# Batch 1's first head pair loaded alone ahead of the output weights, and visits and transposes of token tile 0 placed anew

## Chip, cores and metric

The kernel runs on one core of one Trainium2 chip. The metric is the device time of one execution in microseconds, the lower the better. The kernel before takes 364.70 us (median of 3 executions, 364.70 to 365.26).

## The reference

Block-causal attention for 8 batches of 8 heads (576 tokens, head size 64), then a feed-forward layer with a gated ReLU on the 4608 tokens. Cut to what matters:

```python
scores = q @ k.T / sqrt(64)                 # per batch and head, 576 x 576
scores = where(block_i >= block_j, scores, -1e9)   # blocks of 64 tokens
attn = softmax(scores) @ v
x = attn, heads side by side                # 4608 x 512
out = (relu(x @ w_gate) * (x @ w_val)) @ w_out     # 512 -> 1536 -> 512
```

## The kernel before: the parts that matter

TensorE does everything that can be done as a matmul, and is meant never to stand still. The feed-forward layer goes through the tokens in tiles of 512 (tile 0 is batch 0's first 512 tokens, tile 1 batch 1's, and so on). While TensorE works on tile 0, the attention of batch 1 is put in between its matmuls. The places are given by hand: each matmul of a tile is a step, 144 to a tile. Steps 0 to 95 of a tile are the gate and value products, steps 96 to 143 the output product. An event `(p, f)` puts `f` before step `p`.

The heads go in pairs. Batch 1 has the pairs r = 4, 5, 6, 7; its pair number inside the batch is `hp` = 0, 1, 2, 3. (The prediction says "pair 1's k" and "pair 2" by `hp`, and "visits 5, 6, 7" and "pair 7" by r.) For each pair:

1. `mains_1(hp)`: TensorE transposes q and k into PSUM; VectorE copies q out (`qTm`) and ScalarE copies k out (`kTm`).
2. The visit: TensorE makes the scores, ScalarE takes exponentials of them (two of 128x256, two of 128x1024).
3. `head_av` twice, or `both_av`: the products with v; VectorE normalises each head (a reciprocal and a multiplication).
4. `pe_xT`: TensorE transposes the result, ScalarE (for pair 7 VectorE) copies it out as `xT`, which the next tile reads.

The last 64 tokens of a batch (the 576 are 512 and 64) are its *tail*; they have transposes and visits of their own, which matter here only by their places in tile 1 (`pe_tails`). A *running sum* is one that TensorE is still adding up in PSUM.

```python
psum_sc  = tile_pool(bufs=2)   # scores
psum_one = tile_pool(bufs=1)   # one bank
psum_ffn = tile_pool(bufs=3)   # three banks, shared by the feed-forward sums, one
                               # 128x256 piece of a visit's scores, head_av, transposes
# ... cut
def round_at(p, r, av, to_xT, after=(6, 13)):
    # visit r at step p, products with v at av, transposes at to_xT[0]
    # ... cut
def mains_1(hp):
    if hp == 3:
        both = psum_one.tile([128, 1024], BF, name="one")
        # ... cut
    e1.pe_mains(hp, (dve, act), two)

# loads, in order of issue on SyncE's queue
e1.load_qk(0, 4)                               # q, k of pairs hp 0 and 1: 1 MB
ffn(24)
w_out = [load_w_out(i) for i in range(3)]      # wo: 3 MB
e1.load_v(0, 4)
for h0 in (4, 6):
    e1.load_qk(h0, 2)                          # hp 2, hp 3
e1.load_v(4, 4)
# ... cut
events = round_at(96, 4, (122, 122.1), (126, pe_xT), (6, 11))
events += round_at(112, 5, (130, 130.1), (136, pe_xT), (4, 14))
events += round_at(127.5, 6, (140, 141), (146, pe_xT), (4, 9))
events += round_at(140.5, 7, (150.5, None), (155, pe_xT), (3, 8))
```

The loads come as 32-bit numbers into staging buffers; GpSimd, and in some places VectorE and ScalarE, cast them to bf16.

The softmax here doesn't subtract the row's maximum and nothing guards it: scores larger than these inputs give would overflow.

## Time and profile before

| | before |
|---|---|
| time, median | 364.70 us |
| TensorE busy | 98% |
| granted clock of TensorE | full in all slices |
| start of the scores of visits 4, 5, 6, 7 | 39.38, 43.85, 49.75, 54.89 us |
| start of visit 8 (batch 2) | 74.62 us |
| gaps over 0.12 us in the matmul stream, 30 to 64 us | 2.32 us |
| last matmul's start to the end | 3.72 us |

The granted clock is the share of the full clock that TensorE was allowed, as the profile records it.

Where I give a gap, it is worked out from the records of the trace: the start of one matmul to the start of the next, less 0.417 ns for each column of the first (512 columns 0.213 us). The 0.417 is this trace's own: matmuls of 128 and of 512 columns that follow each other without a wait start 0.056 and 0.216 us apart (medians), 0.160 us for 384 columns. The busy time of matmuls cannot show it, since each record is longer (0.38 us) than its distance to the next.

From the page of the kernel before, the busy times (engine, us, share of the span, instructions), and the rows of TensorE and its clock in 40 slices, in tenths:

```profile
PE 355.3 (98%) x2965; PEld 176.1 (49%) x2965; DVE 168.2 (46%) x394; ACT 168.8 (47%) x280; POOL 112.3 (31%) x147
PE   7999999999999999999999999999999999999996
PEclk9999999999999999999999999999999999999999
```

TensorE runs at full clock and is the limit for most of the span (before 47 us the loads are too, as the result shows). The chain of waits of the same kernel (the work that ended last, followed back from the last instruction to whatever released each step; start, us, what) has near its end:

```profile
297.22 20.72 PE ffnp L593 x96
317.94 10.36 PE ffnp L678 x48
```

96 matmuls in 20.72 us are 0.216 us each: nothing shorter is seen in this trace, so I expect no gain there. What is to be gained lies in the first 64 us. TensorE's timeline of the kernel before (start, us, engine, line, operation, what from what, how many; in brackets the idle time and what ended it) around the output product of tile 0:

```profile
40.03 3.88 PE L678 MATMUL ffnp<-wo,hT 128*128 128x512 bf16 x16
43.85 0.28 PE L399 MATMUL one<-qTm,kTm 64*128 64x256 bf16 x1
...
44.50 2.53 PE L678 MATMUL ffnp<-wo,hT 128*128 128x512 bf16 x10
47.22 0.47 PE L512 MATMUL one<-v_bf,attnT 128*128 128x65 bf16 x10 [0.19 <-POOL v_bf L181]
```

Sixteen matmuls would take 3.46 us, but the next group starts 3.82 us later. 0.1 of the difference is the switch to matmuls of 64 rows, which is found at every visit; 0.26 is a wait for a cast of wo in the middle of the group. The ten that follow lose 0.20 in the same way, and 0.36 (0.19 of it beyond the last matmul's own record) before the first product with v, L512. And at the start of tile 1:

```profile
58.43 0.77 PE L512 MATMUL sc<-v_bf,attnT 128*128 128x65 bf16 x20
59.63 0.61 PE L593 MATMUL sc<-xT,wv 128*128 128x512 bf16 x2 [0.43 <-DVE xnat L478]
...
60.95 0.38 PE L593 MATMUL sc<-xT,wv 128*128 128x512 bf16 x1
61.62 0.59 PE L593 MATMUL ffnp<-xT,wg 128*128 128x512 bf16 x2 [0.30 <-DVE xT L559]
```

Twenty products of 65 columns last 0.60 us, so the next matmul could start at 59.04; it starts 0.59 us later, since it writes to the scores' PSUM buffer that VectorE's normalisation of pair 7 (L478) still reads. Then 0.46 us pass until pair 7's `xT` is there.

### The profile page before, as it was taken

To read this page: it belongs to the slowest core of one execution; us is meant where nothing else is said; L and a number is where in the kernel's file an instruction comes from. 1 tells how busy PE (TensorE), PEld (TensorE's weight loads), DVE (VectorE), ACT (ScalarE), POOL (GpSimd) and SP (SyncE) were. 2 spreads that over 40 slices of the span, in tenths; PEclk is the share of its full clock that TensorE was granted. 3 is DMA by queue.
4 is the path that set the end of the run, shared out by engine and by line. 5 is a ranking of instruction groups with operands and counts; after the bars stand their busy time and mean duration, and the time that the engine had idled before them with its cause. 6 is when DMAs were issued, how large, how long until landed. Compare 5 with 4: busy or idle time off the path is not lost.

```text
span 362.9 us, 7464 instructions
## 1 busy us (share of the span) xinstructions
PE 355.3 (98%) x2965; PEld 176.1 (49%) x2965; DVE 168.2 (46%) x394; ACT 168.8 (47%) x280; POOL 112.3 (31%) x147
## 2 busy tenths in 40 slices
PE   7999999999999999999999999999999999999996
PEld 3644455554554455444544454445544454444443
DVE  4844465566534443554454434543455434333432
ACT  5853655587046643663256624564355333302310
POOL 6756656489138100850057003900000000000000
PEclk9999999999999999999999999999999999999999
DMA  8999999999999992999389963999100420031014
GB/s 254 286 357 374 310 220 293 198 110 174 177 205 123 143 170 81 80 132 177 117 56 144 147 134 55 143 136 152 64 17 14 74 81 0 0 89 29 0 39 108
DMA packets 150387, 49.58 MB, mean 137 GB/s; under 512 B 132816, under 2 KB 143312, under 8 KB 150352
## 3 DMA queue, kind: packets, MB, share of 16 engines
q0 software_dynamic: 70320, 8.85, 52.1%
q1 hardware_dynamic: 74944, 31.47, 42.2%
q10 hardware_dynamic: 5088, 8.78, 7.6%
q8 instruction: 23, 0.38, 0.4%
q14 instruction: 12, 0.10, 0.1%
HBM read 37.75 MB, written 9.44 MB: 130 GB/s over the span
## 4 chain that ended last, share of the span: by engine, by line
PE 85%; DMA 9%; SPq 2%; POOL 1%; DVE 0%; issue 0%; ACT 0%; POOLq 0%; ACTq 0%
PE ffnp L593 46%; PE ffnp L678 24%; PE ffnp L512 5%; DMA stage<-in_k_dram 4%; PE sc L399 3%; DMA stage<-in_moe_w_val_dram 3%; PE ffnp L492 3%; DMA stage<-in_v_dram 3%; SPq L139 2%; PE one L399 2%; PE sc L433 1%; POOL v_bf L181 0%; PE one L433 0%; PE one L593 0%; PE ffnp L260 0%
## 5 line engine op out<-in xcount | busy, mean ns | idle before, releaser
L609 DVE TENSOR_TENSOR hT<-gate_sb,ffnp 128x512 bf16<-128x512 bf16 x106 | 72.7, 687 | 100.5 <-PE ffnp L593 72.1
L603 ACT ACTIVATE gate_sb<-ffnp 128x512 bf16<-128x512 f32 x103 | 61.8, 602 | 88.5 <-PE ffnp L593 88.5
L678 PE MATMUL ffnp<-wo,hT 128*128 128x512 bf16 (+2 forms) x444 | 101.5, 373 | 0.1
L593 PE MATMUL ffnp<-xT,wv 128*128 128x512 bf16 x376 | 99.9, 379 | 0.0
L593 PE MATMUL ffnp<-xT,wg 128*128 128x512 bf16 x364 | 98.2, 379 | 0.4 <-DVE xT L559 0.3
L593 PEld LDWEIGHTS <-wg 128*128 128x128 bf16 x432 | 40.0, 98 | 46.1 <-issue 3.5
L593 PEld LDWEIGHTS <-wv 128*128 128x128 bf16 x432 | 39.8, 98 | 45.3 <-issue 2.3
L678 PEld LDWEIGHTS <-hT 128*128 128x128 bf16 x444 | 40.5, 98 | 42.9 <-issue 1.7
L408 ACT ACTIVATE attnT<-sc 128x1024 bf16<-128x1024 f32 x56 | 56.9, 1039 | 0.0
L282 POOL DMA_DIRECT2D q_bf<-in_q_dram x20 | 17.7, 900 | 92.0 <-DVE hT L609 78.4
L688 DVE COPY ob<-ffnp 128x512 f32<-128x512 f32 (+2 forms) x37 | 25.0, 677 | 40.2 <-PE ffnp L678 40.1
L512 PEld LDWEIGHTS <-attnT 128*128 128x128 bf16 x640 | 25.9, 98 | 15.6 <-DVE xnat L478 3.8
L414 ACT ACTIVATE attnT<-one 128x256 bf16<-128x256 f32 x28 | 10.7, 384 | 35.8 <-PE ffnp L399 35.3
L477 DVE RECIPROCAL recip<-ffnp 128x4 f32<-128x4 f32 (+1 forms) x72 | 12.9, 180 | 29.7 <-PE ffnp L512 20.2
L512 PE MATMUL ffnp<-v_bf,attnT 128*128 128x65 bf16 x560 | 26.1, 194 | 0.0
L478 DVE TENSOR_TENSOR xnat<-ffnp,recip 128x256 bf16<-128x256 f32 x56 | 23.8, 425 | 1.9
L282 POOL DMA_DIRECT2D v_bf<-in_v_dram x25 | 21.3, 898 | 1.3 <-PE ffnp L593 1.0
L454 ACT ACTIVATE attnTt<-one 64x256 bf16<-64x256 f32 x8 | 3.0, 378 | 35.7 <-PE ffnp L433 35.7
L282 POOL DMA_DIRECT2D k_bf<-in_k_dram x20 | 17.7, 927 | 0.2 <-issue 0.2
L399 PE MATMUL sc<-qTm,kTm 64*128 64x512 bf16 (+1 forms) x168 | 16.9, 305 | 0.0
L399 PEld LDWEIGHTS <-kTm 64*128 64x128 bf16 x224 | 9.1, 94 | 14.8 <-issue 11.3
L445 ACT ACTIVATE attnTt<-sc 128x1024 bf16<-128x1024 f32 x16 | 15.7, 1014 | 0.0
(97 smaller groups left out, 251.6 us busy)
## 6 DMA issues: line engine op xcount, KB each, us to landing
out_dram<-ob ACTq DMA_DIRECT2D x29, 256.0 KB, 3.1
stage<-in_moe_w_gate_dram SPq DMA_DIRECT2D x6, 512.0 KB, 9.0
stage<-in_moe_w_val_dram SPq DMA_DIRECT2D x6, 512.0 KB, 9.1
stage<-in_moe_w_out_dram SPq DMA_DIRECT2D x6, 512.0 KB, 10.2
q_bf<-in_q_dram POOLq DMA_DIRECT2D x20, 128.0 KB, 5.4
k_bf<-in_k_dram POOLq DMA_DIRECT2D x20, 128.0 KB, 6.1
v_bf<-in_v_dram POOLq DMA_DIRECT2D x20, 128.0 KB, 7.1
stage<-in_v_dram SPq DMA_DIRECT2D x19, 128.0 KB, 5.0
```

Source lines behind the costliest of these rows:

```text
L282: ins = nc.gpsimd.dma_start(dst, src[b, :, 128 * c : 128 * c + n, :].rearrange("h p d -> p h d"),)
L399: nc.tensor.matmul(where[c].rearrange("p (c n) -> p c n", n=128), kTm[b % 2][head_of(hh), c, hp, :], qTm[b % 2][head_of(hh), c:4, hp, :], ...
L408: return lambda: nc.scalar.activation(at[:, :, lo : lo + 512], sc, AF.Exp, scale=scale)
L445: return lambda: nc.scalar.activation(at[:, :, 2 * i : 2 * i + 2, 0:256], main[i].rearrange("p g (h n) -> p g h n", h=2), AF.Exp, scale=scale,
L477: nc.vector.reciprocal(recip, av[:, :, 64])
L478: nc.vector.tensor_tensor(out=out, in0=av[:, :, 0:64], in1=recip.to_broadcast([rows, n, 64]), op=AX.mult,)
L512: nc.tensor.matmul(av[:, p, :], at[:, col : col + 128], v_bf[b % 2][:, c, h, :], start=(p == 0), stop=(c == p), skip_group_check=True,)
L593: nc.tensor.matmul(to, (wg, wv)[t][f // 4][:, c, 128 * (f % 4) : 128 * (f % 4) + 128], x[:, c], start=(c == 0), stop=(c == 3),)
L603: nc.scalar.activation(gate_sb, gate, AF.Relu)
L609: nc.vector.tensor_tensor(out=h, in0=gate_sb, in1=val, op=AX.mult)
L678: nc.tensor.matmul(op, hT[f][:, 128 * s : 128 * (s + 1)], wo[f // 4][:, f % 4, n0:n1], start=(f == 0), stop=(f == 11),)
L688: nc.vector.tensor_copy(ob, op)
```

## The change

Its intent: wo, for which TensorE waits, shall land earlier; q and k of the second and third pair, which are needed later, go behind it; and the visits are moved to fit. Pair 7, whose result tile 1 waits for, is finished two steps sooner.

```diff
-        e1.load_qk(0, 4)
+        e1.load_qk(0, 2)
         ffn(24)
         w_out = [load_w_out(i) for i in range(3)]
+        e1.load_qk(2, 2)
+        e1.load_qk(4, 2)
         e1.load_v(0, 4)
-        for h0 in (4, 6):
-            e1.load_qk(h0, 2)
+        e1.load_qk(6, 2)
         e1.load_v(4, 4)
 # ... cut: the casts in the same order; q and k of pair 1 cast on their own
-            if hp == 3:
+            if hp >= 2:
                 both = psum_one.tile([128, 1024], BF, name="one")
-            e1.pe_mains(hp, (dve, act), two)
+            e1.pe_mains(hp, (dve, dve if hp == 2 else act), two)
-        events = round_at(96, 4, (122, 122.1), (126, pe_xT), (6, 11))
-        events += round_at(112, 5, (130, 130.1), (136, pe_xT), (4, 14))
-        events += round_at(127.5, 6, (140, 141), (146, pe_xT), (4, 9))
-        events += round_at(140.5, 7, (150.5, None), (155, pe_xT), (3, 8))
+        events = round_at(96, 4, (129, 129.1), (135, pe_xT), (6, 11))
+        events += round_at(124, 5, (136, 136.1), (141, pe_xT), (4, 9))
+        events += round_at(131, 6, (142, 143), (146, pe_xT), (4, 9))
+        events += round_at(139, 7, (148, None), (153, pe_xT), (3, 8))
-            (92, lambda: mains_1(1)),
-            (123.5, lambda: mains_1(2)),
-            (132.5, lambda: mains_1(3)),
+            (117, lambda: e1.cast_qk(2, 2, (None, dve))),
+            (120, lambda: mains_1(1)),
+            (126, lambda: mains_1(2)),
+            (134, lambda: mains_1(3)),
 # ... cut: the first product of pair 4 goes to psum_ffn instead of psum_one
-            (16, lambda: e0.pe_tails((dve, act))),
-            (20, lambda: e1.pe_tails((dve, act))),
+            (20, lambda: e0.pe_tails((dve, act))),
+            (22, lambda: e1.pe_tails((dve, act))),
```

More of the change, by code (lines that the diff above doesn't have):

```diff
@@ L527, in head_av @@
         xnat = xnats[r]
-        if (b > 0 or hh == 1) and (r, hh) != (4, 0):
+        if b > 0 or hh == 1:
             av = psum_ffn.tile([128, 4, 65], FP, name="ffnp")
@@ L821 @@
         cast_w(halves[:1], pool)
-        e1.cast_qk(0, 4, (pool, None))
+        e1.cast_qk(0, 2, (pool, None))
         cast_w(w_out[0], pool)
@@ L827 @@
         cast_w(last_w[:1], pool)
+        e1.cast_qk(2, 2, (pool, None))
+        e1.cast_qk(4, 2, (pool, pool))
         e1.cast_v(0, 4, pool)
-        for h0 in (4, 6):
-            e1.cast_qk(h0, 2, (pool, pool))
+        e1.cast_qk(6, 2, (pool, pool))
         e1.cast_v(4, 4, pool)
@@ L923, in mains_1 @@
                 ]
-            e1.pe_mains(hp, (dve, act), two)
-        events = round_at(96, 4, (122, 122.1), (126, pe_xT), (6, 11))
-        events += round_at(112, 5, (130, 130.1), (136, pe_xT), (4, 14))
-        events += round_at(127.5, 6, (140, 141), (146, pe_xT), (4, 9))
-        events += round_at(140.5, 7, (150.5, None), (155, pe_xT), (3, 8))
+            e1.pe_mains(hp, (dve, dve if hp == 2 else act), two)
[3 more added lines that the diff above has]
+        events += round_at(139, 7, (148, None), (153, pe_xT), (3, 8))
         events += [
             (67, lambda: cast_w(halves[1:], act)),
-            (80, lambda: e1.cast_qk(0, 4, (None, dve))),
+            (80, lambda: e1.cast_qk(0, 2, (None, dve))),
             (90, lambda: mains_1(0)),
-            (92, lambda: mains_1(1)),
             (112.05, lambda: cast_w(last_w[1:], dve)),
-            (123.5, lambda: mains_1(2)),
-            (132.5, lambda: mains_1(3)),
+            (117, lambda: e1.cast_qk(2, 2, (None, dve))),
+            (120, lambda: mains_1(1)),
+            (126, lambda: mains_1(2)),
+            (134, lambda: mains_1(3)),
             (128, lambda: mains_2(0)),
```

## The prediction

("The skill" in it is the Trainium skill.)

> **What bounds it now.** TensorE's matmul stream: busy 98% (table of busy times), 85% of the chain of waits. From 297 us on that chain has 96 matmuls of 512 columns in 20.72 us, 0.216 us each, back to back; the Trainium skill (TensorE: Matmul & The Clock Gate, "Back-to-back issue gap") gives the same 216 ns. The granted clock is full in all slices. So only time in which the stream stands still can be won. From the starts of successive matmuls in TensorE's timeline I find about 5 us of that before 20 us (untouched), about 2.3 us between 37 and 63 us, and later nothing but 0.1 us at each switch between 128-row and 64-row matmuls.
>
> The 2.3 us: 0.18 (k transpose of batch 1's second pair waits for its PSUM bank), 0.26 and 0.20 (output product waits for the casts of wo rows f=6 and f=10), 0.36 (first product with v, at 47.2 us, waits for GpSimd's cast of v), 0.59 (token tile 1 waits for VectorE's normalisation of pair 7), 0.46 and 0.26 (tile 1 waits for xT of pair 7).
>
> **What the change does.** Bytes and matmuls stay; a 512-column k cast costs VectorE about 0.43 us, a 1024-column one 0.69. It moves things:
> - wo lands one q/k pair earlier: 512 KB, 1.4 to 1.5 us at the 350 to 385 GB/s of those slices. The two wo waits (0.46) should nearly vanish; but TensorE gets there earlier too, as visit 5 and pair 1's transposes no longer stand before it, so f=10 may still wait 0.2.
> - v lands about 1.5 us later, cast done near 48.6; its first product moves from step 122 to 129, near 48.5. A wait of 0.0 to 0.4 remains. (v comes in 256-byte pieces; the skill, DMA: Bandwidth & Descriptors, "Specifications", asks 512 B for line rate, and GB/s does dip to 220 at 45 to 54 us.)
> - Pair 7's normalisation and xT come two steps, 0.43 us, earlier relative to tile 1: its waits (1.31) should fall to about 0.3.
> - Visits 5, 6, 7 are squeezed from steps 112, 127, 140 to 124, 131, 139. Each gives ScalarE 2.5 us of exponentials (0.28+0.28+0.98+0.98). With the copies of kTm and xT (0.5 each) ScalarE gets about 10 us of work in the 10.5 us before tile 1; VectorE gets both copies of pair 2 (0.6 each). New waits: pair 1's k and visit 5 on VectorE's late cast and copy (0.3 each); the products of pairs 5 and 6 on PSUM buffers that ScalarE frees late (up to 1 and 0.5).
>
> **On the critical path.** Taken away: about 1.9 us. Newly made: 1 to 2.5 us. Walking both instruction orders with durations, rates and landing delays read from the trace (an estimate) gives +0.1 to +0.5 us; that walk overstates the present kernel's small waits. I take about 0.
>
> **Predicted: 364.6 us, 8 in 10 between 363.5 and 365.8. Faster by over 2%: 0.01; within 2%: 0.98; slower by over 2%: 0.01.**
>
> **What would show it.** The wo waits near 42 and 45 us gone or 0.2; v's cast starting near 47.6; the gap at the start of tile 1 under 0.3; new gaps of 0.3 to 1 us before the products of pairs 5 and 6, ScalarE busy almost without break from 46 to 57 us. After 64 us both timelines alike, shifted by under 1 us.
>
> **What would make it wrong.** ScalarE keeping up (then 363.3); v landing much later than one pair's time; staging buffers coming free later and holding back batch 2's loads, which would show after 60 us.

## The result

| | before | changed |
|---|---|---|
| time, median | 364.74 us | 365.57 us |
| lowest to highest | 364.70 to 365.26 (4) | 365.43 to 365.79 (4) |
| ratio to before | | 1.002, 95% interval 1.0003 to 1.0037 |
| start of visits 4, 5, 6, 7 | 39.38, 43.85, 49.75, 54.89 | 38.84, 46.51, 50.04, 54.91 |
| start of visit 8 | 74.62 us | 74.99 us |
| gaps over 0.12 us, 30 to 64 us | 2.32 us | 2.51 us |
| last matmul's start | 359.18 us | 359.55 us |
| last matmul's start to the end | 3.72 us | 4.07 us |

A ratio is the mean time of one kernel's runs over the mean of the other's runs of the same rounds, so it is not quite the ratio of the medians. Executions over 1.5% slower than the fastest of the same kernel are left out of the means. The changed kernel is 0.8 us slower, 0.2%: the same by the measure of 2%, but outside the spread of the undisturbed runs. The difference of the two profiled executions, 0.72 us, has two parts: 0.37 us until visit 8, which then stays as it is to the last matmul, and 0.35 us after the last matmul.

The page of the changed kernel shows nothing of it (PE still 98%, the clock full):

```profile
PE 355.1 (98%) x2965; PEld 175.4 (48%) x2965; DVE 168.7 (46%) x396; ACT 168.4 (46%) x279; POOL 112.6 (31%) x148
PE   6999999999999999999999999999999999999995
```

**The first part: the matmul stream.** From the first feed-forward matmul (16.25 and 16.27 us) to visit 8 both traces have 522 matmuls. Before this takes 58.37 us with 2.32 us in gaps over 0.12, after 58.72 us with 2.64. So the account closes: the old waits were replaced by new ones that are 0.3 us longer. (0.13 of the 2.64 lies before 30 us. Of the 2.32, 1.5 us were taken away and 0.8 stayed; 1.7 us are new.)

The chain of waits shows something that the prediction passed over. Its last load in the kernel before, and then in the changed one, with the cast that follows:

```profile
40.40 5.57 DMA stage<-in_v_dram
46.11 1.06 POOL v_bf L181
```

```profile
33.06 9.57 DMA stage<-in_moe_w_out_dram
42.69 0.88 POOL wo L340
```

Up to 47.17 us in the kernel before, it is the landing of v that sets the time. So, as I read the chain, TensorE's waits ahead of that (0.18, 0.26 and 0.20) could not be won by themselves; without them TensorE would have waited longer for v. Only what it waits after the last load on the chain is lost for certain.

TensorE's timeline of the changed kernel, for the stretch that answers to that of before:

```profile
39.49 5.57 PE L678 MATMUL ffnp<-wo,hT 128*128 128x512 bf16 x24
44.90 0.39 PE L239 MATMUL sc<-ident,q_bf 128*128 128x128 bf16 x4
...
48.05 0.81 PE L678 MATMUL ffnp<-wo,hT 128*128 128x512 bf16 x3
48.91 0.77 PE L512 MATMUL ffnp<-v_bf,attnT 128*128 128x65 bf16 x20
...
52.66 0.46 PE L512 MATMUL ffnp<-v_bf,attnT 128*128 128x65 bf16 x10
53.85 0.48 PE L512 MATMUL ffnp<-v_bf,attnT 128*128 128x65 bf16 x10 [0.74 <-DVE xnat L478]
...
56.74 0.38 PE L678 MATMUL ffnp<-wo,hT 128*128 128x512 bf16 x1
57.33 0.46 PE L512 MATMUL ffnp<-v_bf,attnT 128*128 128x65 bf16 x10 [0.21 <-ACT xT L559]
```

The output product waits for wo once, 0.22 us. The first product with v waits 0.21. But between the two heads of pair 5 TensorE now stands for 0.90 us, and before the second head of pair 6 for 0.38. At the start of tile 1, the waits that the change was after are nearly gone: the sc sum comes 0.16 us after its place, and no wait for pair 7's `xT` is left. But tile 1 begins at 57.85, and two new waits lie in its first steps: 0.25 before pair 6's transposes (58.53) and 0.18 before pair 7's products (59.38). So its first steps wait 0.59 us in all, where they waited 1.31.

```profile
58.53 0.40 PE L558 MATMUL one<-ident,xnat 128*128 128x128 bf16 x4
...
59.38 0.78 PE L512 MATMUL sc<-v_bf,attnT 128*128 128x65 bf16 x20
60.00 0.60 PE L593 MATMUL ffnp<-xT,wv 128*128 128x512 bf16 x2
60.59 0.61 PE L593 MATMUL sc<-xT,wv 128*128 128x512 bf16 x2
```

What holds TensorE between the heads of pair 5 is seen in the timeline of VectorE and ScalarE in the changed kernel:

```profile
52.33 0.69 DVE L248 COPY qTm<-one 128x512 bf16<-128x512 bf16 x1
53.06 0.58 ACT L248 COPY kTm<-one 128x512 bf16<-128x512 bf16 x1 [1.07 <-DVE qTm L248]
53.16 0.18 DVE L477 RECIPROCAL recip<-ffnp 128x4 f32<-128x4 f32 x1
53.37 0.42 DVE L478 TENSOR_TENSOR xnat<-ffnp,recip 128x256 bf16<-128x256 f32 x1
53.54 0.59 ACT L559 COPY xT<-ffnp 128x512 bf16<-128x512 bf16 x1
```

The last of the first head's products starts at 52.92; VectorE normalises them until 53.79; the second head starts at 53.85. So the second head writes into the very PSUM buffer that the first head has just left, and waits for a full round trip through VectorE. (The records name the semaphores too: the second head's first weight load waits for S101, which VectorE's normalisation updates, and not for S106, which ScalarE's copies update.) Another of the three `psum_ffn` buffers was not to be had, as I read the code: one holds the running output sum, the other the transposes of pair 4, which ScalarE copies out until 54.13 only, because its copy of `kTm` stood in front, which itself waited for VectorE's `qTm`. Before the second head of pair 6 it is ScalarE's copy: it copies out pair 5's `xT` at 56.68, behind an exponential, though the transposes were issued from 56.00 on, and TensorE goes on at 57.33:

```profile
55.77 1.03 ACT L408 ACTIVATE attnT<-sc 128x1024 bf16<-128x1024 f32 x1
56.68 0.61 ACT L559 COPY xT<-ffnp 128x512 bf16<-128x512 bf16 x1
```

This second reading was not tested alone; in e7, where VectorE makes that copy, the gap is gone, but places were moved there too.

ScalarE has become fuller in this stretch, but it is not full. From the table of stretches (length, then busy us and instructions of each engine, clock, DMA share, GB/s), before and after:

```profile
46.00:57.00 11.00, 10.81 (x128) 6.59 (x127) 6.91 (x21) 7.09 (x13) 7.40 (x11) 1.00 0.86 201
```

```profile
46.00:57.00 11.00, 10.22 (x120) 5.88 (x119) 6.04 (x18) 8.18 (x15) 6.57 (x10) 1.00 0.85 201
```

The columns after the length are PE, PEld, DVE, ACT and POOL: ACT goes from 7.09 to 8.18 us of 11, PE from 10.81 to 10.22. ScalarE even stands idle for 1.07 us just before its copy of `kTm`, waiting for VectorE. So what makes its copy of `xT` late is the order in its queue, and not that it has too much to do. By the releasers in the trace, four of the five gaps from 53 to 61 us (0.90, 0.25, 0.18, 0.16) end with VectorE, and 0.38 with ScalarE.

**The second part: the end.** What SyncE waits for after 358 us, before and after (engine, line, what for: us, times, longest):

```profile
SPq L1006 <- DMA out_dram<-ob: 1.2, 2, 1.0
SPq L1006 <- PEq L1006: 0.7, 2, 0.5
```

```profile
SPq L1009 <- DMA out_dram<-ob: 1.6, 1, 1.6
SPq L1009 <- PEq L1009: 0.6, 2, 0.5
```

L1006 and L1009 are the same place, the end of the program. Before, SyncE waits for stores in two pieces; after, in one piece. The records of SyncE there (us after the start of the last matmul, and the hardware DMA semaphore that the wait names; the first wait names none) show why:

```
before   1.15 -   1.22 S100  1.28 S102  1.34 S103  1.40 S104  2.41 S105  2.47 S107  2.75 S108  2.82 S109
changed  1.15 -   2.75 S100  2.81 S102  2.88 S103  2.94 S104  3.00 S105  3.06 S107  3.12 S108  3.18 S109
```

SyncE closes the program with nine waits in a fixed order, 0.06 us each. The last two stores end at the same time in both kernels (the wait that they end is at 2.75). Before, they signal S108 and S109, the last of the row, and one wait follows. After, they signal S100 and S102, and seven follow. The DMAs on the hardware queues take the eight semaphores in turn. The kernel before issues 168 of them, the changed one 170.

### The profile page after: what moved, and what is told of

It is laid out like the page before. It is cut to its first block, busy times and chain, and to the rows that moved or that the text cites. A ratio compares the mean times of both kernels' runs of the same rounds, so it can differ in the third digit from the quotient of the medians.

```text
span 363.6 us, 7469 instructions
## 1 busy us (share of the span) xinstructions
PE 355.1 (98%) x2965; PEld 175.4 (48%) x2965; DVE 168.7 (46%) x396; ACT 168.4 (46%) x279; POOL 112.6 (31%) x148
## 4 chain that ended last, share of the span: by engine, by line
PE 86%; DMA 10%; SPq 1%; ACT 1%; DVE 0%; POOL 0%; issue 0%; POOLq 0%
PE ffnp L593 46%; PE ffnp L678 25%; PE ffnp L512 5%; PE sc L399 3%; DMA stage<-in_moe_w_gate_dram 3%; PE ffnp L492 3%; DMA stage<-in_moe_w_out_dram 3%; DMA stage<-in_moe_w_val_dram 3%; PE one L399 2%; SPq L139 1%; DMA stage<-in_v_dram 1%; PE sc L433 1%; DMA stage<-in_k_dram 1%; PE one L433 0%; PE sc L593 0%
```

## The experiments

The theories at the start: **S**, the order of loads does what it should, and its gain is eaten because the visits are squeezed, so that PSUM buffers come back late, above all from ScalarE's queue. **L**, late v costs the time. **T**, the gain at the start of tile 1 only mirrors waits earlier. **D**, the moved transposes of the tails matter. **E**, the 0.35 us at the end hang on the number of DMAs alone. The experiments ran in three sets (e0 to e3, e4 to e7, e8 to e11), each on one chip with its own runs of the kernel before. Some executions there were disturbed (2 to 6 us longer, most of them at a mean clock of 0.994 to 0.998). All but two of them count, so the intervals of the ratios are wide and most contain 1; where they do, I read the medians, the lowest times, and the traces. The traces' gaps at PSUM buffers repeat within 0.05 us where neither their places nor their copies were changed; the waits for wo do not (0.46 in the kernel before, none in e5, which has the same stream; 0 to 0.32 in the changed kernel and its variants). The profiled executions of e3 and e7 are disturbed ones (365.62 and 368.50 us): they stand still for over 2 us near 110 and 111 us, after the stretch that is read here. Comparisons between sets are between chips. The places in e6, e7 and e11 were found by the walk of dependences that the prediction describes; the chip's runs decide.

In the table, the last column is the time from the last matmul's start to the end.

| run | this, median (lowest) | before on that chip, median (lowest) | ratio, 95% interval | visit 8 | gaps 30 to 64 us | end |
|---|---|---|---|---|---|---|
| e0 changed again | 365.77 (365.33) | 365.16 (364.45) | 1.000, 0.996 to 1.004 | 74.73 | 2.42 | 4.07 |
| e1 kTm of pair 7 by VectorE | 365.33 (365.09) | same | 1.0008, 0.9959 to 1.0056 | 74.26 | 1.98 | 4.07 |
| e2 new places, old loads | 366.71 (366.53) | same | 1.0026, 0.9986 to 1.0066 | 75.90 | 3.50 | 3.69 |
| e3 pair 7's part alone | 364.05 (363.60) | same | 0.9969, 0.9916 to 1.0023 | 73.52 | 1.01 | 3.73 |
| e4 changed, six more stores | 365.07 (364.96) | 364.69 (364.51) | 1.0021, 0.9996 to 1.0046 | 74.70 | 2.26 | 3.70 |
| e5 before, two more stores | 365.11 (364.82) | same | 1.0029, 0.9993 to 1.0066 | 74.48 | 1.86 | 4.07 |
| e6 before, mended | 363.84 (363.56) | same | 0.9976, 0.9964 to 0.9988 | 73.85 | 1.43 | 3.71 |
| e7 changed, mended | 364.65 (364.25) | same | 1.0012, 0.9979 to 1.0045 | 74.06 | 1.70 | 3.71 |
| e8 changed, old tail places | 365.70 (365.42) | 364.97 (364.60) | 1.0015, 0.9982 to 1.0047 | 74.83 | 2.72 | 4.06 |
| e9 v ahead of pair 2 | 366.17 (365.97) | same | 1.0024, 0.9993 to 1.0056 | 75.51 | 3.30 | 4.07 |
| e10 xT of pair 4 by VectorE | 365.57 (365.37) | same | 1.0010, 0.9973 to 1.0047 | 74.53 | 1.88 | 4.07 |
| e11 before, mended again | 363.65 (363.53) | same | 0.9958, 0.9933 to 0.9984 | 73.61 | 1.23 | 3.70 |

All outputs were correct.

### e0: the changed kernel again

No edit.

> The changed kernel once more, in five rounds, so that the experiments beside it have it on their own chip. Its loss against the kernel before was 0.8 us in time, but the two traces are only 0.37 us apart up to the last matmul. If the rest (0.4 us after the last matmul) is chance, the difference measured here falls towards 0.4 us; if it belongs to the change, it stays at 0.8 us.

Median 0.6 and lowest 0.9 us above the kernel before; the end is 4.07 us again. So the end belongs to the change. Visit 8 is 0.11 us later than in the trace of the kernel before; in the first trace of the changed kernel it was 0.37. Chance lies there: the gaps over 0.12 us sum up to 2.42 us here, to 2.64 in the first execution (0.13 of which, before 30 us, is missing here).

### e1: the k copy of pair 7 by VectorE

```diff
-            e1.pe_mains(hp, (dve, dve if hp == 2 else act), two)
+            e1.pe_mains(hp, (dve, dve if hp >= 2 else act), two)
```

> The changed kernel, with the one copy of kTm of head pair 3 of batch 1 given to VectorE instead of ScalarE. Theory S (the gain was eaten by ScalarE: its queue stands behind that copy, which waits for VectorE, and so the xT copy of pair 4 frees its PSUM buffer late): the gap of 0.90 us between the two heads' products of pair 5, near 52.9 us, shrinks to about 0.3, and the kernel gains 0.5 to 0.7 us over the changed one. Rival L (the order of the loads costs the time: v comes late and holds back what follows): nothing about v changes here, so the kernel stays within 0.2 us of the changed one, and the time won before pair 5 is lost again at a later wait.

The gap at 52.8 us fell from 0.90 to 0.32, visit 8 came 0.47 us sooner than in e0, and the median and the lowest time fell by 0.44 and 0.24 us. Theory S named the place and the size of the gap; the time won is less than the 0.5 to 0.7 us expected. Visit 8 comes 0.36 us sooner than in the kernel before, with the feed-forward matmuls starting at the same time (16.22 and 16.25): 0.58 us less in this one gap more than undoes the loss of the stream. TensorE's, ScalarE's and VectorE's timeline of this kernel:

```profile
52.45 0.58 ACT L559 COPY xT<-ffnp 128x512 bf16<-128x512 bf16 x1 [0.67 <-PE ffnp L558]
52.46 0.46 PE L512 MATMUL ffnp<-v_bf,attnT 128*128 128x65 bf16 x10
52.85 0.68 DVE L248 COPY kTm<-one 128x512 bf16<-128x512 bf16 x1
53.08 0.46 PE L512 MATMUL ffnp<-v_bf,attnT 128*128 128x65 bf16 x10 [0.16 <-ACT xT L559]
...
53.65 0.43 DVE L478 TENSOR_TENSOR xnat<-ffnp,recip 128x256 bf16<-128x256 f32 x1
```

With the copy of `kTm` out of its queue, ScalarE copies pair 4's `xT` at 52.45 instead of 53.54. And now the second head waits for that copy, no longer for the first head's normalisation: it starts a full microsecond before that normalisation ends (54.08), and its records name S106, ScalarE's semaphore. So the program was built with another buffer for it, the one of pair 4's transposes.

### e2: the new places with the old loads

The loads and casts are in the order of the kernel before (pairs 0 and 1 together ahead of wo, cast together); the events are those of the changed kernel without the separate cast at step 117.

> The changed kernel's places for visits, transposes and products, with the loads and casts in the order of the kernel before (pairs 0 and 1 loaded and cast together ahead of wo, then wo, v, pairs 2, 3). Rival L: v is 1.5 us earlier than in the changed kernel and the wait before its first product is gone, so this is as fast as the changed kernel or faster. Theory S: the two halves of the change belong together. The new places let TensorE reach the output product earlier, while wo lands as late as before, so the two waits for wo grow from 0.26 and 0.20 to about 0.9 and 0.5 us, the ScalarE waits stay (0.9 and 0.4), and the kernel is 1.0 to 1.5 us slower than the changed one.

0.9 us slower than e0 in the median, 1.17 us later at visit 8. The waits for wo are 0.20 and 0.98 (I had them as 0.9 and 0.5: in sum 1.18 instead of 1.4), the pair 5 and 6 gaps are again 0.90 and 0.38. So the new order of loads is worth about a microsecond to the new places, and L is wrong in its strong form. The end, 3.69 us, is that of the old loads: 168 DMAs.

### e3: pair 7's part alone, on the kernel before

```diff
-        events += round_at(140.5, 7, (150.5, None), (155, pe_xT), (3, 8))
+        events += round_at(139, 7, (148, None), (153, pe_xT), (3, 8))
-            (16, lambda: e0.pe_tails((dve, act))),
-            (20, lambda: e1.pe_tails((dve, act))),
+            (20, lambda: e0.pe_tails((dve, act))),
+            (22, lambda: e1.pe_tails((dve, act))),
```

> The kernel before, with only the last part of the change: visit 7 at step 139, its products at 148, its transposes at 153, and the transposes of the tails at 20 and 22. Theory S: here ScalarE has room, so the gain that the changed kernel shows at the start of token tile 1 (waits of 0.59, 0.46 and 0.26 us down to 0.2 to 0.3 in all) is kept, with about 0.4 us of new wait at visit 7; 0.6 to 0.9 us faster than the kernel before. Rival T (the start of tile 1 is not where the changed kernel gains; its gain there only mirrors waits earlier): within 0.2 us of the kernel before.

1.1 us below the kernel before in the median, 0.85 in the lowest; visit 8 at 73.52 instead of 74.62. Of the three waits at the start of tile 1 (1.31 us) 0.16 is left, and 0.35 is new before visit 7. Rival T falls. These few lines take away 1.15 of the 1.5 us that the whole change takes away. TensorE's timeline of e3 around the new wait and the start of tile 1:

```profile
54.36 0.28 PE L399 MATMUL one<-qTm,kTm 64*128 64x256 bf16 x1 [0.18 <-ACT kTm L248]
...
58.52 0.60 PE L593 MATMUL ffnp<-xT,wv 128*128 128x512 bf16 x2
59.12 0.60 PE L593 MATMUL sc<-xT,wv 128*128 128x512 bf16 x2
```

Part of the 1.1 us is chance: in this execution the waits for wo did not show, because the feed-forward matmuls started at 16.53 instead of 16.25, and the loads were no later for it. The trace of e5 below allows for that: it has the stream of the kernel before, also started late (16.64) and shows no waits for wo. From the first product with v to visit 8, the kernel before takes 27.40 us, e5 27.40, and e3 26.56. So the lines win 0.84 us. (The interval of e3's ratio contains 1, because of disturbed executions; the gain rests on the traces and the lowest times.)

### e4 and e5: the number of DMAs

Stores of a 128-row block are cut into two of 64 rows, for six blocks in e4 and for two in e5:

```diff
 # e4, on the changed kernel
-            n = 64 if j == B - 1 and s < 3 else 128
+            n = 64 if j in (5, 6, B - 1) and s < 3 else 128
 # e5, on the kernel before
-            n = 64 if j == B - 1 and s < 3 else 128
+            n = 64 if (j == B - 1 and s < 3) or (j == 6 and s < 2) else 128
```

> The changed kernel; six of its output stores, of token tiles 5 and 6, are cut in two halves, so it issues 176 hardware DMAs instead of 170. Nothing else is touched, and the bytes are the same. Theory E (the end): SyncE closes the program with nine waits on semaphores, in a fixed order, 0.06 us each; the DMAs take the eight DMA semaphores in turn, and with two more loads than before the last two stores fall on the two that are waited for early in that row, so that seven waits still follow when the stores have landed. 176 is 168 (the kernel before) plus eight, so the last stores fall on the last two again: from the last matmul to the end 3.72 us instead of 4.07, the matmul stream as in the changed kernel, the time 0.35 us below the changed kernel. Rival (the 0.35 us belong to chance or to the smaller loads): the end stays at 4.07.

> The kernel before, with two of its output stores, of token tile 6, cut in two halves: 170 hardware DMAs, as the changed kernel has. Theory E: from the last matmul to the end 4.07 us instead of 3.72, the matmul stream as in the kernel before; 0.35 us slower than the kernel before. Rival (chance, or the loads): the end stays at 3.72.

From the last matmul to the end e4 takes 3.70 us and e5 4.07. SyncE's waits after 358 us, first e4, then e5:

```profile
SPq L1009 <- DMA out_dram<-ob: 1.2, 2, 0.9
```

```profile
SPq L1006 <- DMA out_dram<-ob: 1.6, 1, 1.6
```

e4 waits as the kernel before does, e5 as the changed kernel does. Theory E is shown both ways, and the other traces agree: the seven with 168 or 176 DMAs end 3.69 to 3.73 us after the last matmul's start, the seven with 170 end 4.06 to 4.07 after it. In time, e5 is 0.4 us above the kernel before (medians); e4 is 0.4 us above it, which is what the stream loses, and 0.5 to 0.7 us below the changed kernel on other chips.

### e6 and e7: versions made to be faster

e6 is the kernel before with places moved by mostly at most three steps; the main ones are `mains_1(1)` at 90.5, pair 5's visit at 112.5, its products at 128 and 129.1, its xT at 138, visit 7 at 139.5 with its products at 147.5 and its transposes at 153.5, pair 7's q copied by ScalarE and k by VectorE. e7 is the changed kernel with pair 7's k copied by VectorE (as in e1) and pair 6's by ScalarE, the xT copies of pair 5 by VectorE and of pair 7 by ScalarE, places moved by up to two steps, the tails back at 16 and 19.5, and e4's six stores.

> A version meant to beat both: the loads of the kernel before, with only small moves of places. The transposes of pair 1 at 90.5, pair 5's products at 128 and 129.1, its xT at 138, pair 3's q copied by ScalarE and its k by VectorE, visit 7 at 139.5 with its products at 147.5 and its transposes at 153.5, the second tails at 18. Theory S says where room is: the waits at the start of tile 1 (1.31 us) vanish but for some 0.3 us before pair 7's products, and the waits on wo shrink; 1.1 to 1.6 us faster than the kernel before, so 0.2 to 0.6 us faster than the experiment with the part of pair 7 alone. Rival L (the order of loads is what matters): no more than 0.9 us.

> The changed kernel's order of loads, with places chosen so that neither ScalarE's nor VectorE's queue holds a PSUM buffer back (k of pair 3 to VectorE and of pair 2 to ScalarE, xT of pair 5 to VectorE and of pair 7 to ScalarE, places moved by up to two steps), and with the six cut stores. Theories S and E together: the gap of 0.90 us is gone or under 0.25, the sum of the waits between 37 and 63 us is about 1.5 us instead of 2.5, and the end is 3.72 us: 1.2 to 1.5 us faster than the changed kernel, 0.4 to 0.9 faster than the kernel before. It stays behind the version with the old loads, since v, which lands 1.5 us later, sets when pair 4's products can start. Rival L in its strong form (late v alone costs the time): no more than 0.4 us, the end, is won over the changed kernel.

e6 is 0.85 us faster than the kernel before, clear of noise, though less than expected; it is no better than e3. Its transposes of pair 1 at step 90.5 came too early and waited 0.62 us for their PSUM buffer. e7 is 0.9 to 1.1 us faster than the changed kernel (expected 1.2 to 1.5), and level with the kernel before (expected 0.4 to 0.9 faster): a miss in size. The 0.90 us gap is gone, and the 0.38 too, but 0.42 us at pair 1's k, 0.40 before pair 7's products and 0.25 before pair 6's transposes remain, beside three of 0.20 to 0.23. With waits mended as far as I could, the order of loads of the change brought nothing over the old one.

### e8: the tails back at their old steps

```diff
-            (20, lambda: e0.pe_tails((dve, act))),
-            (22, lambda: e1.pe_tails((dve, act))),
+            (16, lambda: e0.pe_tails((dve, act))),
+            (20, lambda: e1.pe_tails((dve, act))),
```

> The changed kernel with the transposes of the two batches' tails back at steps 16 and 20 of token tile 1 (the change has them at 20 and 22). If this part matters for the result (rival D), the kernel moves by over 0.3 us. Theory S: the tails' PSUM buffer comes 0.1 to 0.2 us too early at most, one gap of up to 0.2 us comes back near 62 us, and the kernel stays within 0.2 us of the changed one; the wait of 0.26 us that the kernel before has there belongs to pair 7, not to the tails.

The time is the changed kernel's; visit 8 is 0.1 us later than in e0. D falls. One detail of mine was wrong: the gap of 0.26 us came back in full (at 62.96 us; 62.74 in the kernel before), so it belongs to the tails' early place and not to pair 7's `xT`.

### e9: v ahead of pair 2

```diff
         e1.load_qk(2, 2)
-        e1.load_qk(4, 2)
         e1.load_v(0, 4)
+        e1.load_qk(4, 2)
         e1.load_qk(6, 2)
 # and the casts in the same order
```

> The changed kernel with v loaded and cast ahead of q and k of pair 2 instead of behind them. Rival L (late v costs the time): v lands about 1.5 us sooner, the wait of 0.2 us before the first product with v goes, and the kernel is 0.2 us or more faster than the changed one. Theory S: v was only 0.2 us too late, since the change also moved its first use; now pair 2 lands about 2 us later and its transposes wait, 0.6 to 1.0 us in sum near 48 us, the ScalarE gaps (0.90, 0.38) stay, and the kernel is 0.5 to 0.9 us slower than the changed one.

0.5 us slower than e8 on the same chip, 0.78 us later at visit 8 than e0. The wait for v is gone; pair 2's transposes wait 0.46 and 0.33 us instead; 0.90 and 0.38 stay. L falls: v was late by 0.2 us, no more.

### e10: pair 4's xT by VectorE

```diff
-            to_xT_pe(r, dve if r % 4 == 3 else act)
+            to_xT_pe(r, dve if r in (4, 7) else act)
```

> The changed kernel with the one copy of xT of pair 4 (128x512) given to VectorE instead of ScalarE. Theory S in its exact form: the products of the second head of pair 5 write into the PSUM buffer that this copy reads, and the copy waits in ScalarE's queue behind the copy of kTm of pair 3. By VectorE it no longer does: the gap of 0.90 us falls to 0.3 to 0.45, visit 7 comes 0.4 to 0.6 us sooner against the first output product, and the kernel is 0.4 to 0.6 us faster than the changed one. If the buffer is not the reason (the gap waits for exponentials or for v), the gap stays at 0.9.

The gap fell from 0.90 to 0.53, less than the 0.30 to 0.45 that I expected, and the time cannot be told from the changed kernel's (0.13 us below e8 in the median, 0.05 in the lowest). TensorE and VectorE in this kernel:

```profile
52.28 0.69 DVE L248 COPY qTm<-one 128x512 bf16<-128x512 bf16 x1
52.53 0.46 PE L512 MATMUL ffnp<-v_bf,attnT 128*128 128x65 bf16 x10
52.89 0.41 DVE L559 COPY xT<-ffnp 128x512 bf16<-128x512 bf16 x1
53.36 0.46 PE L512 MATMUL ffnp<-v_bf,attnT 128*128 128x65 bf16 x10 [0.36 <-DVE xT L559]
```

Here too the second head got the buffer of pair 4's transposes, and starts as that copy ends, which now stands behind VectorE's `qTm`. With e1 this settles what kind of wait it is: whoever reads the buffer last sets the start, be it VectorE's normalisation (changed kernel), ScalarE's copy (e1) or VectorE's copy (e10). My exact form of S, that in the changed kernel it is ScalarE's copy, is wrong: that copy ends at 54.13, and TensorE goes on at 53.85.

### e11: the mended kernel before, once more

e6 with `mains_1(1)` back at step 92.

> The mended version of the kernel before once more, with the transposes of pair 1 back at step 92, since at 90.5 they waited 0.62 us for their PSUM buffer. Theory S: that gap falls to 0.2; what is won comes back in part as waits for wo (0.0 to 0.5) where the loads land late, so 0.9 to 1.5 us faster than the kernel before, that is 363.2 to 363.8 us where the kernel before takes 364.7.

363.65 us, where the kernel before takes 364.97 on the same chip (364.70 elsewhere); ratio 0.9958, clear of noise. The gap at pair 1's transposes is 0.18 as expected, and 0.14 at wo and 0.37 at v are what is left of the loads. It beats both kernels; it has no lead over e3 that these runs could show.

## Why the prediction was right

The time, 365.57 us, lies in the range, nearly a microsecond above the middle, and within 2%. Point by point:

- **What bounds it**: right after 47 us. Before that the loads do, so the two waits for wo of the kernel before (0.46) should not have been counted as time to be won. After visit 8 both streams run alike, 0.37 us apart up to the last matmul.
- **wo**: right. 0.46 us of wait fell to 0.22, and GpSimd's first cast of wo starts 1.4 us sooner (35.89 instead of 37.30).
- **v**: right. Its cast starts at 47.80 (I said 47.6), and the first product waits 0.21 us (0.0 to 0.4).
- **Start of tile 1**: right for the old waits, 1.31 us to 0.16 (about 0.3 predicted); one of them (0.26) was put down to pair 7 and belonged to the tails (e8). Two new ones in the same first steps, 0.25 before pair 6's transposes and 0.18 before pair 7's products, were not foreseen, so only 0.72 us were won there.
- **New waits**: the sizes for pairs 5 and 6 ("up to 1 and 0.5") were 0.90 and 0.38. Pair 1's k waits 0.20 (0.3); visit 5's 0.3 did not come. The cause was half right: for pair 6 it is ScalarE's copy; for pair 5 it is a buffer used twice in a row, so a full round trip through VectorE, and ScalarE's lateness only explains why the other buffer was not free.
- **ScalarE's load**: wrong. "Busy almost without break from 46 to 57 us" was forecast, with about 10 us of work in the 10.5 us before tile 1; measured are 8.18 us of 11, and 8.16 of those 10.5. It is the order of its queue that counted, not the amount.
- **The sum**: about 1.9 us were to go and 1 to 2.5 to come; 1.5 went and 1.7 came. The walk gave +0.1 to +0.5 us, and the stream measured +0.37 (+0.1 in e0). I took "about 0" instead, because the walk overstates the small waits of the kernel before. The walk was the better number.
- **What was overlooked**: "Bytes and matmuls stay" is true, but the number of DMAs does not stay, and "After 64 us both timelines alike, shifted by under 1 us" is true only up to the last matmul. I counted the two extra DMAs as free, and they cost 0.35 us at the end, half of the whole loss, which e4 and e5 take away and bring back.
- **Luck**: that the time still lies in the range. The range had no term for the end; it held because it was wide enough (its upper edge is 365.8; the slowest execution took 365.79, and e0 on another chip has a median of 365.77).

What stays open: how much of the stream's loss is chance. In the traces, visit 8 of the kernel before (and of e5, which has its stream) is at 74.62 and 74.48, that of the changed one (and of e4) at 74.99, 74.73 and 74.70: 0.1 to 0.5 us later. The start of the feed-forward matmuls varies between 16.07 and 16.68 us over the profiled executions, and where it is late the waits for wo shrink. What follows the last load on the chain repeats: the 27.40 us of the kernel before are the same in e5, though one has waits for wo and the other none.

## What to carry to other kernels

When an instruction stream is full, moving work may only trade one wait for another; list the waits that a new place makes beside those that it takes away, and for a product that alternates between two results ask which PSUM buffer the second gets and who reads it last. Try the parts of such a change one by one: here a few lines (e3) won 0.84 us of the stream, and with the rest of the change this was lost again. And count the DMAs: a change that moves no byte more can still lengthen the end of the program, if the last store signals a semaphore that is waited for early.

## What the Trainium skill lacked or had wrong

- No page has the end that these traces show: SyncE waits for the DMA semaphores one by one, 0.06 us each, so that the end takes 3.72 us with 168 or 176 hardware DMAs and 4.07 with 170 (other remainders by eight were not tried). "Runtime: NRT & Kernel Launch" (section "The ~15µs preamble/postamble breakdown") gives about 1.5 us for the first barrier after the kernel, and nothing for such waits at the kernel's own end.
- "TensorE: Matmul & The Clock Gate", section "Back-to-back issue gap", gives both 216 ns for a single 512-column matmul and about 131 ns for a sustained stream of weight load and matmul. This trace has the stream at 216 ns (96 in 20.72 us), each with its own weight load; 131 is not seen. It also gives about 81 ns at 128 columns; the four transposes of 128 columns from 51.56 us on in the changed kernel are followed 0.22 us later by the next, 55 ns each. (They come in short runs; a long stream of that size is not in these traces.)
- "Perfetto Trace Analysis", section "Optimization Strategy", says that consistent bubbles can mean too few PSUM buffers. Here the bubble came once, not as a repeating gap, and it was that shortage all the same (0.90 us; 0.32 in e1, where the second head got another buffer); the page's advice in the same section, to find the semaphore that is waited for and the instruction that updates it, is what found it.
